# Recurrent attention, Mish layer and greedy experts: later bonuses on VectorE, a gate that counts four columns at a time, and its branch behind the experts

## The chip, the cores and the metric

The kernel runs on one core of a Trainium2 chip. Its engines have queues of their own: TensorE (PE; its weight loads are PEld), VectorE (DVE), ScalarE (ACT), GpSimd (POOL), and SyncE (SP), which issues most transfers; POOL issues the gathers and scatters. They meet at semaphores. The metric is the device time of one execution in microseconds.

## The reference

Three stages follow one another. The first is a linear recurrence over 768 steps for 4 x 8 heads of width 48, the second a dense layer over 3072 tokens, the third a mixture of 8 experts, where each token goes to one expert and each expert takes 384 tokens, picked greedily by the size of the logits.

```python
for t in range(S):
    cur = np.einsum('bhd,bhe->bhde', u[None] * kt, vt)
    y[:, :, t] = np.einsum('bhd,bhde->bhe', rt, state + cur)
    state = wt[:, :, :, None] * state + np.einsum('bhd,bhe->bhde', kt, vt)

h = x @ w_in
g = h * np.tanh(np.log1p(np.exp(h)))            # h above 20 is taken as it is
x = g @ w_out

order = np.argsort(-(x @ w_gate).flatten())
for idx in order:                               # largest logit first
    tok, e = idx // E, idx % E
    if assigned[tok] >= 0 or counts[e] >= cap: continue
    assigned[tok] = e; counts[e] += 1
for e in range(E):
    out[assigned == e] = np.maximum(x[assigned == e] @ w1[e], 0) @ w2[e]
```

The term with `u` is the bonus: step t's own key and value enter y with the weight sum over d of r*u*k, one number for each token and head.

## The kernel before

All matmuls of the two layers run on float16 halves: each operand is split into a high and a low part, and three products (high*high, high*low, low*high) stand for one. One list of events, sorted by keys from a table of numbers (`CFG`), fixes the order in which the instructions are written out; each engine works through its own in that order.

*Attention.* The sequence is cut into 24 units of 128 rows (two batches of 64 steps). A unit goes through the steps `att0`, `r1`, `k1` (decays, scaled r and k on VectorE), `bon1`, `bon2` (the bonus), `K`, `A1`, `S`, `y`. For the bonus, `att0` multiplies r and k of the unit in their transposed layout (line 353), `bon1` sums over d with eight small float32 matmuls against `u_T` (line 374) and moves the result to SBUF (`bT`), `bon2` transposes it on TensorE (line 381), moves it again (`bt`) and spreads it over a diagonal `Dt` (line 387). `CFG["dve"]` says for which units or pieces VectorE and for which ScalarE does such a move.

*Dense layer.* 12 groups of 256 tokens; `mm1` (line 561) makes the hidden tiles, VectorE and ScalarE the activation, and `mm2` (line 616) the output, in a stream of steps (`mm2_stream`): a step is three matmuls of 128x384, or 128x392 where eight columns carry the gate's logits. The stream's steps are strewn between the other work as fillers (`more(n)`); how many remain for the gate is set by `CFG["rate"]` and `CFG["beat"]`.

*Gate* (`gate`, `count`). Instead of sorting, seven phases look for the threshold at which the next expert is full, by 32-way search: four rounds in the first phase, three in each later one, 22 counts. In a count VectorE compares the tokens' values with 32 grid points (`compare`, two halves, line 839), TensorE adds up, by 24 matmuls of 32 columns of weights, how many tokens of each expert lie above each point (`tally`, line 844), VectorE compares with the free places (`ge`, line 858), TensorE spreads the result to all partitions (line 861) and VectorE takes the maximum (line 862). At each `yield` fillers from the stream are put in, `CFG["amount"]` steps of three. `aside` holds pieces of VectorE work (the low half of the first expert's weights, line 1095; the assignment of the last phase) that are put into a count, one at a time.

*Indices* (`make_idx`). A token's slot is turned into two one-hot matrices, `Q` (slot over 128) and `OH` (slot modulo 128, times the token's number), whose product over 24 matmuls is the list of tokens by expert; `check` counts whether every expert has 384. Then the first gathers go out, every engine loads the check's result into a register (line 1206) and branches (line 1207) around `exact_gate`, which is run when the check fails. Thirty dummy matmuls (`hold`, line 1214) stand ahead of the experts.

*Experts.* For each of 8: gather the rows (line 1116), transpose (1128), two matmul layers (1150, 1167), scatter (1172), with the next expert's weights split in between.

Of the kernel before, what the change touches and what calls it, by code (L numbers as in the profile page):

```python
# [18 lines left out]
P = 128  # L19
# [4 lines left out]
CFG = {'conv': [-28.468, -27.682, -10.675, -9.847, -2.299, 2.231, 3.277, 4.9, 3.919, 5.933, 7.595, 7.755, 8.526, 9.471,  # L24
          10.454, 11.547],
 'split': [-25.675, -27.076, -3.646, 1.639, 1.676, 2.567, 3.66, 7.281, 4.908, 7.502, 8.011, 9.047, 9.415, 10.573,
           10.811, 12.671],
 'ogT': [5.845, 8.719, 9.555, 9.756, 11.048, 11.752, 12.058, 13.442],
 'ogM': [7.704, 9.381, 9.717, 10.657, 11.711, 12.133, 12.863, 15.308],
 'u': ({'att0': -6.475,  # L30
        'bon1': -2.417,
        'bon2': -1.013,
        'r1': 0.465,
        'k1': -1.596,
        'K': 1.584,
        'A1': 2.502,
        'S': 3.903,
        'y': 3.747},
       {'att0': -2.581,
        'bon1': -0.459,  # L40
        'bon2': 0.009,
        'r1': -0.43,
        'k1': 0.751,
        'K': 5.062,
        'A1': 5.181,
        'S': 5.915,
        'y': 5.938}),
 'un': {0: {'att0': -24.666,
            'r1': -16.321,
            'bon1': -15.996,  # L50
            'k1': -21.723,
            'K': -15.816,
            'A1': -14.582,
            'bon2': -15.13,
            'S': -15.595,
            'y': -13.813},
        1: {'att0': -20.054,
            'r1': -19.91,
            'bon1': -18.88,
            'k1': -18.572,  # L60
# [3 lines left out]
            'S': -16.313,  # L64
            'y': -15.386},
        2: {'att0': -21.397,
            'r1': -20.207,
            'bon1': -20.059,
            'k1': -19.864,
            'bon2': -3.587,  # L70
            'K': 4.356,
            'A1': 3.2,
            'S': 6.8,
            'y': 7.301},
        3: {'att0': -21.601,
            'r1': -18.499,
            'bon1': -0.615,
            'k1': -16.885,
            'bon2': 2.966,
            'K': 3.773,  # L80
            'A1': 6.657,
            'S': 6.652,
            'y': 7.118},
        4: {'K': 5.178,
            'A1': 4.914,
            'S': 5.604,
            'y': 8.165,
            'att0': 0.318,
            'bon1': 1.82,
            'bon2': 4.604,  # L90
            'r1': 3.684,
            'k1': 4.536},
        5: {'y': 7.557,
            'att0': -2.858,
            'bon1': 3.509,
            'bon2': 3.642,
            'r1': 3.498,
            'k1': 1.649,
            'K': 6.184,
            'A1': 5.986,  # L100
            'S': 6.749},
        6: {'att0': -3.536, 'bon1': -2.54, 'bon2': 0.136},
        7: {'att0': -2.822, 'bon1': -0.422, 'bon2': 1.839}},
 'rate': [(17, 1), (16, 18), (77, 192), (80, 194), (96, 224), (99, 245)],
 'beat': (16, 82, (8, 3, 1, 1, 1, 0, 3, 5)),
 'close_cv': 15.533,
 'close_att': 86.65,
# [11 lines left out]
           ('ld', 5): -25.319,  # L119
           ('ld', 6): -18.857,  # L120
           ('ld', 7): -23.785,
           ('ld', 8): -21.26,
           ('ld', 9): -20.908,
           ('warm', 1): -24.585,
           ('warm', 2): -22.903,
           ('warm', 3): -6.441,
           ('warm', 4): 9.117,
           ('warm', 5): 2.921,
           ('warm', 6): 3.3},
 'warm': [3, 0, 3, 21, 0, 2, 8],  # L130
 'amount': {'I0': 3, 'I1': 0, 'c': 3, 'g': 1, 'o': 20, 't': 5},
# [7 lines left out]
         'ghi': {2, 4, 5, 6, 7, 9, 10, 14, 17, 18, 19, 22, 26, 27, 30, 31, 34, 35, 38, 39, 42, 43, 46, 47},  # L139
# [7 lines left out]
 'alone': {9},  # L147
 'lg': 8.022,
 'hold': 30,
 'xq': set(),  # L150
 'cvn': 2}
# [3 lines left out]
def tile_rwkv_mish_greedy_moe(  # L155
# [3 lines left out]
    v: bass.AP,  # L159
    u: bass.AP,  # L160
    w_in: bass.AP,
# [7 lines left out]
    NU, C, H, D = v.shape  # L169
# [44 lines left out]
    UN = [divmod(n, NCH) for n in range(NU)]  # L214
    vt = {}
# [17 lines left out]
    def load_v(n):  # L233
        if n >= NU:
            return
        vt[n] = pa.tile([P, H, D], F32, name="v")
        nc.sync.dma_start(vt[n], v[n])
# [19 lines left out]
    u_T = pa.tile([P, NP, 2, 32], F32, name="u_T", bufs=1)  # L257
    nc.sync.dma_start(u_T.rearrange("p a h b -> p (a h b)"), u)
# [82 lines left out]
    def att0(n):  # L341
# [10 lines left out]
        rk = pa.tile([P, NP, C], F32, name="rk", bufs=1)  # L352
        nc.vector.tensor_tensor(rk, Tps["r", n], Tps["k", n], op=ALU.mult)
        rks[n] = rk
# [14 lines left out]
    def bon1(n):  # L369
        pb = pq.tile([P, C], F32, name="Y", bufs=2)  # L370
        for h in range(2):
            t = slice(L * h, L * h + L)
            for p in range(NP):
                nc.tensor.matmul(pb[32 * p:32 * p + 32, t], u_T[:, p, h, :], rks[n][:, p, t], start=True, stop=True)
        bTs[n] = pa.tile([P, C], F32, name="bT", bufs=1)
        move("bT", n, bTs[n], pb)

    def bon2(n):
        pb = pq.tile([P, C], F32, name="Y", bufs=2)
# [3 lines left out]
        move("bT", n, bt, pb.rearrange("t (p j) -> t j p", j=32)[:, 0:2, :])  # L383
        bt = bt.rearrange("t j p -> t (j p)")
# [222 lines left out]
    def mm2_part(g, m, f, n):  # L607
# [7 lines left out]
        for i, (a, b) in enumerate(((0, 0), (0, 1), (1, 0))):  # L615
            nc.tensor.matmul(x, gt[:, a, ff, m * P:(m + 1) * P], wo[:, b, f, 0:n],  # L616
                             start=(f == 0 and i == 0), stop=(f == NF - 1 and i == 2))

# [41 lines left out]
    def mm2_stream():  # L660
        for g in range(NG):
            for m in range(MG):
                for f in range(NF):
                    mm2_part(g, m, f, WO if g < ND0 else DM)
# [52 lines left out]
    def more(n):  # L717
        for _ in range(n):
            next(fill, None)
        done[0] += n  # L720
# [56 lines left out]
    J = 32  # L777
# [46 lines left out]
    cnS = pgt.tile([J, NE], F32, name="cnS")  # L824
    ohj = pgt.tile([J, J], F32, name="ohj")
# [16 lines left out]
    def tally(cn, E_, h):  # L842
        for i in range(h * QT, (h + 1) * QT):
# [476 lines left out]
```

## Time and profile before

| what | value |
|---|---|
| runs shown | 783.0, 784.49, 786.48 us, median 784.49 |
| profiled execution | 783.24 us, span of its instructions 781.5 us |
| PE busy | 733.1 us, 94% of the span |
| DVE busy | 556.6 us, 71% |
| ACT busy | 411.0 us, 53% |
| POOL busy | 57.0 us, 7% |
| mean granted clock of TensorE | 0.981 of full speed |

The span is what the trace covers. Matmuls overlap, so a group's length is read from its start to the start of the next group; its own figure runs to a modelled end and is longer. The weight loads run beside the matmuls.

### The profile page before, as it was taken

How to read it: one execution, taken by the hardware profiler on the slowest of the kernel's cores; microseconds unless marked ns; L12 is line 12 of the kernel's file. 1: busy time of each engine (PE TensorE's matmuls, PEld its weight loads, DVE VectorE, ACT ScalarE, POOL GpSimd, SP SyncE). 2: the span in 40 equal slices, each digit the busy share in tenths (PEclk: the TensorE clock that was granted, in tenths of full speed). 3: DMA queues.
4: the chain of work that ended last, by engine and by line, in shares of the span. 5: the costliest groups of instructions: out<-in, count | busy, mean ns of one | idle time of the engine just before them, and what ended most of it. 6: DMA issues, size and time to landing. Idle time of an engine off the chain costs nothing. (4 is left out here: it accounts for less than half of the span.)

```text
span 781.5 us, 20165 instructions
## 1 busy us (share of the span) xinstructions
PE 733.1 (94%) x8807; PEld 517.0 (66%) x8807; DVE 556.6 (71%) x1054; ACT 411.0 (53%) x689; POOL 57.0 (7%) x98
## 2 busy tenths in 40 slices
PE   3977699999999999999999999999979999999996
PEld 2656576878777787777777765555556666666663
DVE  8999996978788887978777446777745664446620
ACT  3365875576774667667576781110024565445621
POOL 0000000000000000000000010000031223312211
PEclk9998899999999999999999999999989999999999
DMA  8852331323133141322210005100525644456100
GB/s 335 247 181 60 125 97 26 68 42 86 45 67 60 40 94 41 70 57 47 53 27 13 5 14 180 22 21 12 183 74 182 213 150 162 167 200 212 52 31 30
DMA packets 22220, 74.12 MB, mean 95 GB/s; under 512 B 4496, under 2 KB 13072, under 8 KB 20080
## 3 DMA queue, kind: packets, MB, share of 16 engines
q1 hardware_dynamic: 19056, 63.35, 27.7%
q0 software_dynamic: 3072, 9.44, 3.8%
q8 instruction: 71, 1.16, 0.6%
q14 instruction: 21, 0.17, 0.1%
HBM read 62.15 MB, written 9.44 MB: 92 GB/s over the span
## 5 line engine op out<-in xcount | busy, mean ns | idle before, releaser
L561 PE MATMUL Hp<-xg,wi 128*128 128x256 f16 x1728 | 210.4, 277 | 3.9 <-ACT wi L504 1.9
L616 PE MATMUL X<-wo,g 128*128 128x392 f16 (+1 forms) x1152 | 211.0, 328 | 0.0
L561 PEld LDWEIGHTS <-wi 128*128 128x128 f16 x1728 | 167.8, 99 | 33.3 <-ACT wi L504 2.1
L616 PEld LDWEIGHTS <-g 128*128 128x128 f16 x1152 | 107.2, 98 | 63.5 <-issue 0.9
L565 ACT ACTIVATE es<-Hp 128x512 f32<-128x512 f32 x96 | 57.4, 597 | 112.8 <-PE Hp L561 80.0
L1167 PE MATMUL X<-a,hT 128*128 128x384 f16 x576 | 97.2, 326 | 0.0
L1150 PEld LDWEIGHTS <-a 128*128 128x128 f16 x612 | 57.8, 98 | 37.2 <-issue 1.2
L1167 PEld LDWEIGHTS <-hT 128*128 128x128 f16 x576 | 56.4, 98 | 34.8
L1150 PE MATMUL Hp<-xe,a 128*128 128x384 f16 (+1 forms) x468 | 74.7, 314 | 0.7 <-DVE xe L1131 0.4
L588 DVE TENSOR_TENSOR hs<-hs,es 128x1024 f32<-128x1024 f32 x48 | 57.6, 1218 | 17.8 <-ACT es L580 17.6
L601 DVE TENSOR_TENSOR g<-hs,g 128x1024 f16<-128x1024 f32 x48 | 58.7, 1224 | 13.1 <-ACT g L329 12.1
L1095 DVE SCALAR_TENSOR_TENSOR a<-stg,a 128x384 f16<-128x384 f32 (+1 forms) x112 | 63.9, 607 | 0.0
L1092 ACT ACTIVATE a<-stg 128x384 f16<-128x384 f32 (+1 forms) x112 | 56.9, 561 | 0.8 <-DMA stg<-in_w_dram 0.8
L1170 ACT ACTIVATE or<-X 128x384 f32<-128x384 f32 x24 | 11.8, 491 | 81.0 <-issue 60.7
L1155 DVE SCALAR_TENSOR_TENSOR hT<-Hp,hT 128x384 f16<-128x384 f32 x48 | 26.4, 551 | 38.7 <-ACT hT L1154 38.7
L1131 DVE SCALAR_TENSOR_TENSOR xe<-cn,xe 128x384 f16<-128x384 f32 x24 | 13.2, 553 | 56.4 <-ACT xe L1130 56.4
L580 ACT ACTIVATE es<-es,right 128x1024 f32<-128x1024 f32 x48 | 53.3, 1153 | 0.2
L329 ACT ACTIVATE x1o<-X 128x384 f32<-128x384 f32 x19 | 9.4, 493 | 81.2 <-PE X L616 41.6
L329 ACT ACTIVATE hs<-Hp 128x512 f32<-128x512 f32 x77 | 46.0, 598 | 9.0 <-DVE g L601 9.0
L573 ACT ACTIVATE es<-es,mid__124 128x2048 f32<-128x2048 f32 x24 | 48.1, 2003 | 0.4
L1116 POOL DMA_INDIRECT xr<-x_dram,idx x24 | 27.5, 1146 | 119.6 <-DVE idx L1067 111.4
L273 ACT ACT_TABLE_LOAD x26 | 33.4, 1283 | 1.2 <-PEq L1304 0.8
(190 smaller groups left out, 881.1 us busy)
## 6 DMA issues: line engine op xcount, KB each, us to landing
stg<-in_w_dram SPq DMA_DIRECT2D x16, 1536.0 KB, 6.8
T<-in_rkw_dram SPq DMA_DIRECT2D x42, 289.5 KB, 4.9
g<-in_w_out_dram SPq DMA_DIRECT2D x8, 768.0 KB, 5.8
v<-in_v_dram SPq DMA_DIRECT2D x24, 192.0 KB, 3.1
x_dram<-x1o SPq DMA_DIRECT2D x48, 96.0 KB, 2.2
g<-in_w_in_dram SPq DMA_DIRECT2D x4, 768.0 KB, 7.9
wo<-in_w_in_dram SPq DMA_DIRECT2D x4, 768.0 KB, 11.6
xg<-xg SPq DMA_DIRECT2D x72, 16.0 KB, 1.9
```

The lines of the kernel that those rows point to most:

```text
L329: nc.scalar.activation(dst, src, AF.Copy, scale=scale)
L561: nc.tensor.matmul(h[:, fi, :], wi[:, a, kk, f * P:(f + 1) * P], xg[g][:, b, kk, :], start=(n == 0), stop=(n == 3 * KD - 1))
L565: nc.scalar.activation(es[g, hf][:, 2 * q:2 * q + 2, :], h, AF.Tanh, scale=0.5 / (SX * SWI))
L573: nc.scalar.activation(e, e, AF.Arctan, scale=-0.5, bias=mid_)
L580: nc.scalar.activation(e, e, AF.Sin, scale=-2.0, bias=right)
L588: nc.vector.tensor_tensor(h, h, e, op=ALU.mult)
L601: (nc.vector if on_v("glo", 2 * H_ + q) else nc.gpsimd).tensor_tensor(gt[:, 1, sl], h, gt[:, 0, sl], op=ALU.subtract)
L616: nc.tensor.matmul(x, gt[:, a, ff, m * P:(m + 1) * P], wo[:, b, f, 0:n], start=(f == 0 and i == 0), stop=(f == NF - 1 and i == 2))
L1092: nc.scalar.activation(dst[:, 0], src, AF.Copy, scale=sc_)
L1095: nc.vector.scalar_tensor_tensor(dst[:, 1], src, sc_, dst[:, 0], op0=ALU.mult, op1=ALU.subtract)
L1150: nc.tensor.matmul(ps[:, cs], a1[:, a, kk, f * P:(f + 1) * P], x[:, b, kk, cs], start=(n == 0), stop=(n == 3 * KD - 1))
L1167: nc.tensor.matmul(ps, h[:, a, f, ms], a2[:, b, f, :], start=(n == 0), stop=(n == 3 * NF2 - 1))
```

## The change

1. Units 6 to 23 (`nb` is 6) no longer compute their bonus on TensorE. r and k of such a unit are loaded a second time, in the layout with tokens on partitions (`rkn`, 128 x 768 floats, one buffer; `u` repeated on all partitions in `uw`); VectorE multiplies r by k, by u, and sums over d.
2. A count's tally takes four token columns at once: six matmuls with 128 columns of weights and 32 moving columns give all pairs of four, `own` masks the pairs that belong together (a VectorE product into `cm`), and four matmuls with `fold` add the four quarters up. The fillers are now given by single matmuls (`more_third`), with one more place for them (`s`). `aside` pieces stand behind `cm`, or behind `ge` where a phase begins.
3. Index lists use slots over 64 and modulo 64; the token's number goes into `Q`.
4. The register is loaded ahead of the last expert and the branch stands behind it; its body repeats the experts. `check` stands behind the indices, and 70 dummy matmuls where 30 were.
5. The table of numbers is another one throughout (keys, fillers, who does which move).

```diff
- 'amount': {'I0': 3, 'I1': 0, 'c': 3, 'g': 1, 'o': 20, 't': 5},
+ 'amount': {'I0': 8, 'I1': 1, 'c': 8, 'g': 2, 's': 2, 'o': 33, 't': 12},
...
     def bon1(n):
+        if n >= NB:
+            return
...
     def bon2(n):
+        if n >= NB:
+            x = rkn[n]
+            nc.vector.tensor_tensor(x[:, 0], x[:, 0], x[:, 1], op=ALU.mult)
+            nc.vector.tensor_tensor(x[:, 0], x[:, 0], uw, op=ALU.mult)
+            bt = pa.tile([P, 2, NP], F32, name="bt")
+            for j in range(2):
+                nc.vector.tensor_reduce(bt[:, j], x[:, 0].rearrange("t (p j d) -> t j p d", p=NP, j=2)[:, j], op=ALU.add,
+                                        axis=AX.X)
+            rkn.pop(n)
+            load_rk(n + 1)
+            bonus_diag(n, bt)
+            return
...
+    nc.vector.tensor_copy(fold, ident[:, 0:J])
+    for i in range(4):
+        nc.vector.tensor_reduce(own[:, i, 0:1], ident[:, J * i:J * i + J], op=ALU.max, axis=AX.X)
+        if i:
+            nc.vector.tensor_tensor(fold, fold, ident[:, J * i:J * i + J], op=ALU.add)
+        nc.vector.tensor_copy(own[:, i, 1:NE], own[:, i, 0:1].to_broadcast([P, NE - 1]))
...
     def tally(cn, E_, h):
-        for i in range(h * QT, (h + 1) * QT):
-            nc.tensor.matmul(cn, I_[:, i, :], E_[:, i, :], start=(i == 0), stop=(i == NTT - 1))
+        for i in range(h * QT, (h + 1) * QT, 4):
+            nc.tensor.matmul(cn, I_[:, i:i + 4, :], E_[:, i:i + 4, :], start=(i == 0), stop=(i == NTT - 4))
...
-            if h == NH - 1 and aside:
-                aside.pop(0)()
             yield f"I{h}"
-            tally(cn, E_, h)
+            tally(c4, E_, h)
+        nc.vector.tensor_tensor(cm, c4, own, op=ALU.mult)
         if late is not None:
             late()
+        elif aside:
+            aside.pop(0)()
+        yield "s"
+        cn = pgs.tile([P, CAP], F32, name="hx", bufs=1)[0:J, 0:NE]
+        for i in range(4):
+            nc.tensor.matmul(cn, fold, cm[:, i * NE:(i + 1) * NE], start=(i == 0), stop=(i == 3))
         nc.vector.tensor_tensor(ge, cn, remS[0:J, :], op=ALU.is_ge)
+        if late is not None and aside:
+            aside.pop(0)()
         yield "g"
...
+        nc.vector.tensor_tensor(Q, Q, tid[:, :, None].to_broadcast([P, NTT, 2 * NTT]), op=ALU.mult)
...
-            for i in range(q * NTT // NQ, (q + 1) * NTT // NQ):
-                nc.vector.tensor_scalar(OH[:, i], col, slf[:, 1, i:i + 1], tid[:, i:i + 1], op0=ALU.is_equal, op1=ALU.mult)
+            i = slice(q * NTT // NQ, (q + 1) * NTT // NQ)
+            nc.vector.tensor_tensor(OH[:, i], col[:, None, 0:64].to_broadcast([P, NTT // NQ, 64]),
+                                    slf[:, 1, i, None].to_broadcast([P, NTT // NQ, 64]), op=ALU.is_equal)
...
-    redo = nc.values_load(badi, min_val=0, max_val=NE)
-    with tc.If(redo > 0):
-        exact_gate()
-        run_through(make_idx())
-        gather(0)
...
+    experts(lambda: redo.append(nc.values_load(badi, min_val=0, max_val=NE)))
+    with tc.If(redo[0] > 0):
+        exact_gate()
+        run_through(make_idx())
...
+        gather(0)
+        experts()
```

**VectorE around a later unit's diagonal.** Before (`L387` is the diagonal; its `bt` comes from TensorE by way of ScalarE; `L353` is the r*k product):

```order
L350 SCALAR_TENSOR_TENSOR F_144<-T_93,first 128x520
L353 TENSOR_TENSOR rk<-T_93 128x512
L601 TENSOR_TENSOR g<-hs,g 128x1024
L327 TENSOR_SCALAR hs<-Hp 128x512
L458 TENSOR_TENSOR S_142<-S_146,Y 128x4x48 x2
L460 TENSOR_TENSOR S_142<-S_142,F_140 128x8x48
L327 TENSOR_SCALAR xg<-A 128x4x128
L480 SCALAR_TENSOR_TENSOR xg<-A,xg 128x4x64 x2
L397 TENSOR_TENSOR T_92<-T_92,F_140 128x512
L387 TENSOR_TENSOR Dt<-diag,bt 128x512
```

and now, at the same place of the program (`rk` is the tile with tokens on partitions):

```order
L491 TENSOR_TENSOR S_142<-S_146,Y 128x4x48 x2
L493 TENSOR_TENSOR S_142<-S_142,F_140 128x8x48
L339 TENSOR_SCALAR xg<-A 128x4x128
L513 SCALAR_TENSOR_TENSOR xg<-A,xg 128x4x64 x2
L430 TENSOR_TENSOR T_93<-T_93,F_140 128x512
L397 TENSOR_TENSOR rk<-rk 128x384
L398 TENSOR_TENSOR rk<-rk,uw 128x384
L401 TENSOR_REDUCE bt<-rk 128x4 x2
L420 TENSOR_TENSOR Dt<-diag,bt 128x512
```

The r*k product left its place behind the scan, and four instructions that read only loaded data stand directly ahead of the diagonal.

**VectorE in one count of the first phase.** Before (`I_` the compare, `a` a piece of the weights, `ge` the comparison with the free places, `sc` the maximum):

```order
L839 TENSOR_TENSOR I__6877<-best,jk_6837 128x384 x2
L1095 SCALAR_TENSOR_TENSOR a_6907<-stg,a_6907 128x512
L858 TENSOR_TENSOR ge<-cn,remS 32x8
L862 TENSOR_REDUCE sc<-tp 128x1
L909 TENSOR_SCALAR y<-best,sc 128x24
```

and now:

```order
L887 TENSOR_TENSOR I__6718<-best,jk_6678 128x384 x2
L902 TENSOR_TENSOR cm<-cn,own 128x32
L1154 SCALAR_TENSOR_TENSOR a_6763<-stg,a_6763 128x512
L911 TENSOR_TENSOR ge<-hx,remS 32x8
L917 TENSOR_REDUCE sc<-tp 128x1
L964 TENSOR_SCALAR y<-best,sc 128x24
```

The masking product `cm`, which waits for the tally, now stands ahead of the piece of the weights, and `ge` behind both.

**TensorE at the end of the index lists.** Before:

```order
L1065 LDWEIGHTS OH
L1065 MATMUL cn<-Q,OH 128x24
L1206 TENSOR_LOAD badi
L1207 COMPARE_AND_BRANCH
L844 LDWEIGHTS I__6877
L844 MATMUL cn<-Eo,I__6877 32x8
```

and now:

```order
L1123 LDWEIGHTS OH
L1123 MATMUL cn<-Q,OH 64x24
L1011 LDWEIGHTS ones
L1011 MATMUL tp<-cp,ones 128x8
L1268 LDWEIGHTS ones
L1268 MATMUL cn<-tri,ones 128x128
```

The load and the branch around the exact gate (whose first tally stands behind them before) are gone from here; the check's matmul and the dummy matmuls follow the last index matmul directly.

In the program as written out, the stream holds 393 fillers between the first reduction of the range and the experts before, and 396 now.

## Rows read from the trace of the kernel before

**Rows 1.** Busy us (and count) in two stretches: PE, PEld, DVE, ACT, POOL; clock; DMA
```profile
40.00:120.00 80.00, 61.48 (x1026) 49.99 (x1025) 77.24 (x120) 57.06 (x93) 0.00 (x0) 0.87 0.38 111
160.00:450.00 290.00, 288.77 (x4261) 222.70 (x4259) 230.15 (x350) 194.03 (x272) 0.00 (x0) 1.00 0.22 49
```

**Rows 2.** Timeline of PE around one unit's bonus: start us, us, instruction
```profile
319.51 0.43 PE L374 MATMUL Y<-rk,u_T 128*32 128x64 f32 x16
319.87 2.14 PE L561 MATMUL Hp<-xg,wi 128*128 128x256 f16 x18
...
324.98 0.27 PE L381 MATMUL Y<-ident,bT 128*128 128x128 f32 x1
325.09 1.66 PE L616 MATMUL X<-wo,g 128*128 128x392 f16 x9
```

**Rows 3.** Groups of VectorE by form: count, busy us, mean ns, idle before
```profile
L353 DVE TENSOR_TENSOR rk<-T 128x512 f32<-128x512 f32 x24 | 16.0, 667 | 0.5 <-DMA T<-in_rkw_dram 0.5
...
L460 DVE TENSOR_TENSOR S<-S,F 128x384 f32<-128x384 f32 x20 | 11.2, 558 | 0.7
...
L920 DVE TENSOR_REDUCE best<-M 128x24 f32<-128x192 f32 x7 | 2.3, 334 | 0.0
```

**Rows 4.** Timeline where the gate begins
```profile
477.54 0.16 DVE L871 SCALAR_TENSOR_TENSOR wk<-wk 128x1 f32<-128x1 f32 x1
...
478.93 0.27 PE L874 MATMUL tp<-ident,wk 128*1 128x128 f32 x1
```

**Rows 5.** Timeline of one count of the gate
```profile
487.44 0.76 PE L844 MATMUL cn<-Eo,I__6877 128*32 128x8 f16 x24
487.47 0.69 DVE L1095 SCALAR_TENSOR_TENSOR a<-stg,a 128x512 f16<-128x512 f32 x1
...
488.23 0.15 DVE L858 TENSOR_TENSOR ge<-cn,remS 32x8 f16<-32x8 f32 x1
...
488.72 0.17 PE L861 MATMUL tp<-ge,ones 32*128 32x8 f16 x1
...
489.48 1.03 DVE L839 TENSOR_TENSOR I__6877<-y,jk 128x384 f16<-128x384 f32 x2
...
490.40 0.76 PE L844 MATMUL cn<-Eo,I__6877 128*32 128x8 f16 x24
```

**Rows 6.** Timeline: small matmuls with 128 columns of weights
```profile
103.92 0.60 PE L537 MATMUL Y<-wgs,wT 128*128 128x8 f16 x18
```

**Rows 7.** Timeline from the last count to the experts; then landing of the gathers
```profile
558.16 0.17 PE L861 MATMUL tp<-ge,ones 32*128 32x8 f16 x1
...
564.54 0.76 DVE L1054 TENSOR_TENSOR Q<-col,slf 128x576 f16<-128x576 f16 x1
...
571.41 0.18 DVE L1067 TENSOR_SCALAR idx<-sl 128x24 int32<-128x24 int32 x1
...
573.98 0.96 POOL L1116 DMA_INDIRECT xr<-x_dram,idx  x1 [0.30 <-issue]
575.09 3.29 PE L1214 MATMUL cn<-OH,ones 128*128 128x128 f16 x30 [3.93 <-PEq L1207]
578.21 0.83 PE L1128 MATMUL cn<-ident,xr 128*128 128x128 f32 x6
...
DMA to landing us min/median/max: 3.0/3.4/4.3
```

**Rows 8.** Register loads and branches: ns min/median/max, first and last start us
```profile
L1206 PEldq TENSOR_LOAD <-badi x1: 492/492/492, 571.0 to 571.0; - x1
...
L1207 ACTq COMPARE_BRANCH  x1: 50/50/50, 567.8 to 567.8; - x1
...
L1207 PEldq COMPARE_BRANCH  x1: 3359/3359/3359, 571.6 to 571.6; - x1
```

**Rows 9.** The last scatter (timeline), and POOL's drain at the end
```profile
775.68 0.96 POOL L1172 DMA_INDIRECT out_dram<-or,idx  x1 [2.85 <-ACT or L1170]
...
L1315 POOLq DRAIN  x3: 40/113/5199, 775.4 to 781.2; - x3
```

More of the change, by code (lines that the diff above doesn't have):

```diff
@@ L103 @@
[L103 to L106, printed above, removed]
+            'S': -16.335,
+            'y': -15.249},
+        2: {'att0': -21.418,
+            'r1': -19.974,
+            'bon1': -19.617,
+            'k1': -19.64,
+            'bon2': -3.61,
+            'K': 4.997,
+            'A1': 3.276,
+            'S': 6.922,
+            'y': 7.451},
@@ new lines @@
+        3: {'att0': -21.269,
+            'r1': -17.288,
+            'bon1': -0.568,
+            'k1': -15.337,
+            'bon2': 3.561,
+            'K': 3.783,
+            'A1': 6.667,
+            'S': 6.009,
+            'y': 7.234},
+        4: {'K': 5.214,
+            'A1': 4.95,
+            'S': 5.604,
+            'y': 7.836,
+            'att0': 0.608,
+            'bon1': 1.856,
+            'bon2': 4.294,
+            'r1': 3.706,
+            'k1': 4.57},
+        5: {'y': 7.485,
+            'att0': -2.727,
+            'bon1': 3.512,
+            'bon2': 3.756,
+            'r1': 3.755,
+            'k1': 1.907,
+            'K': 6.014,
+            'A1': 5.811,
+            'S': 6.972},
@@ L158, in tile_rwkv_mish_greedy_moe @@
     rkw: bass.AP,
-    v: bass.AP,
+    rkv: bass.AP,
     u: bass.AP,
+    ur: bass.AP,
     w_in: bass.AP,
@@ L1064, in make_idx @@
             for i in range(q * NTT // NQ, (q + 1) * NTT // NQ):
-                nc.tensor.matmul(ix, OH[:, i, :], Q[:, i], start=(i == 0), stop=(i == NTT - 1))
+                for b in range(2):
+                    nc.tensor.matmul(ix[64 * b:64 * b + 64], OH[:, i, :], Q[:, i, b::2], start=(i == 0),
+                                     stop=(i == NTT - 1), skip_group_check=True)
         nc.vector.tensor_scalar(sl, ix, float(-(NT // 2)), float(NT - 1 - NT // 2), op0=ALU.max, op1=ALU.min)
@@ L1193, in tile_rwkv_mish_greedy_moe @@
     for kind in gate():
-        more(amount[kind])
+        more_third(amount[kind])
     while aside:
         aside.pop(0)()
-    for kind in make_idx(check):
-        more(amount[kind])
+    for kind in make_idx():
+        more_third(amount[kind])
+    check()
     more(1000)
@@ L1205, in tile_rwkv_mish_greedy_moe @@
     gather(0)
-    redo = nc.values_load(badi, min_val=0, max_val=NE)
-    with tc.If(redo > 0):
-        exact_gate()
-        run_through(make_idx())
-        gather(0)
-    if CFG["hold"]:
-        hold = pgs.tile([P, P], F32, name="cn")
-        for _ in range(CFG["hold"]):
-            nc.tensor.matmul(hold[:, 0:P], ones, OH[:, 0], start=True, stop=True)
+    hold = pgs.tile([P, P], F32, name="cn")
+    for _ in range(CFG["hold"]):
+        nc.tensor.matmul(hold[:, 0:P], ones, tri, start=True, stop=True)
     pend = {}
@@ L1226, in more_cv, with experts @@
                 conv_lo(*x)
-    for e in range(NE):
-        nx = e + 1 < NE
-        f = 0
-        while f < NF2:
-            k = 2 if e == 0 and f == 0 else 1
-            e_mm1(e, *range(f, f + k), parts=ME if k > 1 else 1)
-            for i in range(f, f + k):
-                if i == 0 and nx:
-                    gather(e + 1)
-                    if e > 0:
-                        load_w(e + 1)
-                if nx:
-                    more_cv(e + 1)
-            f += k
-        more_cv(e + 1, 100)
-        for m in range(ME):
-            if nx:
-                xpose(e + 1, m)
-            e_mm2(e, m)
+    def experts(last=None):
+        for e in range(NE):
+            nx = e + 1 < NE
+            if not nx and last is not None:
+                last()
+            f = 0
+            while f < NF2:
+                k = 2 if e == 0 and f == 0 else 1
+                e_mm1(e, *range(f, f + k), parts=ME if k > 1 else 1)
+                for i in range(f, f + k):
+                    if i == 0 and nx:
+                        gather(e + 1)
+                        if e > 0:
+                            load_w(e + 1)
+                    if nx:
+                        more_cv(e + 1)
+                f += k
+            more_cv(e + 1, 100)
+            for m in range(ME):
+                if nx:
+                    xpose(e + 1, m)
+                e_mm2(e, m)
+    redo = []
+    experts(lambda: redo.append(nc.values_load(badi, min_val=0, max_val=NE)))
+    with tc.If(redo[0] > 0):
+        exact_gate()
+        run_through(make_idx())
+        for d in (pend, wts, wf, xe, hT):
+            d.clear()
+        scat.clear()
+        load_w(0)
+        for x in small_pieces(0):
+            conv_hi(*x)
+            conv_lo(*x)
+        load_w(1)
+        gather(0)
+        experts()
 _OUTS = [((3072, 384), "float32")]
```

204 lines of the change are left out of this document (99 added, 105 removed), and 27 rows, old and new, of the table CFG.

## The prediction

> **What bounds the kernel now.** I read the busy time by stretch first. From 160 to 450 us TensorE is busy for 288.8 of 290 us at the full clock, VectorE for 230 [rows 1]: there time is TensorE work, and a microsecond taken off it is a microsecond. From 40 to 120 us it is the other way round, VectorE 77.2 of 80 and TensorE 61.5 [rows 1]; the change keeps the first six units' bonus as it is and adds nothing to VectorE before that point, so I give this part no gain and no loss. Then the timelines of three places: a unit's bonus, one count of the gate, and the passage from the gate to the experts, where TensorE stands.
>
> **The change part by part.**
>
> *The bonus of units 6 to 23.* In the stream of TensorE the eight products of one unit take from 319.51 to 319.87, 0.36 us, and its transpose from 324.98 to 325.09, 0.11 us [rows 2]. That is 0.47; the durations modelled for the two are 0.43 and 0.27, 0.70 together, but they overlap with their neighbours. I take 0.50 a unit, near the stream's figure: 18 x 0.50 = 9.0 us, all on the engine that bounds. What VectorE takes over: two products of 128x384 at 0.56, two sums over 192 numbers at 0.33, less the 0.67 of the old r*k product [rows 3]: 1.12 + 0.67 - 0.67 = 1.1 us a unit, 20 us in all, of which the new table hands some 7 back to ScalarE (nine moves of the hi half and two of kn, 128x512 each, at the 0.67 of such an instruction [rows 3]). VectorE has 60 us to spare in 160 to 450 [rows 1], so I price this at nothing; with that cover gone the wait could eat the whole 9. At the other end stands 18 x 0.70 = 12.6 us. The r and k rows that are loaded anew are on no path: a load for unit n+1 goes out behind the sums of unit n, some ten of VectorE's instructions ahead of its reader. Behind it on SP's queue stand x1's stores and the loads of later units, which are not due then.
>
> *The gate's start.* Twelve small VectorE instructions that make `fold` and `own` now stand between the read of the last logits and the two reductions of the range. Nothing shows them; by the 0.16 of the smallest one there [rows 4] they are 1.9 us. So the maximum that TensorE transposes is ready at about 479.7 and not at 477.70, where 15 fillers covered it until 478.93 [rows 4]. Twelve fillers end 0.5 earlier: TensorE waits about 1.3 us, and the first compare comes 0.4 us later than before, with seven fillers fewer spent. Bounds -1 (the twelve hidden) to +0.9.
>
> *The 22 counts.* Before, a count takes 2.96 us (487.44 to 490.40), 12 fillers of it [rows 5]. A filler is 0.163 us (nine with 392 columns take 1.66 with one 0.33 us tail [rows 2], scaled to 384). The 24 matmuls are 0.69 us. Their six successors have 128 columns of weights; the nearest row is 18 matmuls of that kind with 8 columns in 0.60, less a tail of 0.17, so 0.025 each [rows 6]. I take 0.17 for six and 0.11 for the four that fold: 0.4 us less TensorE time a count. But the chain grows by a link. From the start of the matmul that spreads the result (488.72) the second compare ends at 490.51, +1.79 [rows 5]. TensorE comes to the second half of the tally at +1.86 (eight fillers, three matmuls, one filler, two changes of 0.1), the masking product on VectorE runs until about +2.31 (0.19, between the 0.15 of a 32x8 instruction and the 0.55 of a 128x384 one [rows 5]), and behind it, ahead of the `ge` that the next matmul needs, stands a piece of the weights, 0.69 for 512 columns [rows 5] or 0.55 for 384 [rows 3]: `ge` ends at +3.12 and the next spread starts at +3.2. Of the sixteen counts that don't open a phase six go like this (+0.24), eight with the smaller piece (3.05, +0.09), two without (2.91): +2.1 us together, with 13 fillers each for 12. The six that open a phase come out even, 4.7 us, but their `assign` now follows `ge` and holds up the next reduction by 0.3: +1.8. Counts: +4 us, while 16 more fillers are done. Bounds: -2 (VectorE never late, TensorE sets 2.9 and the phase openings gain) to +11 (half a microsecond more a count).
>
> *Indices and the branch.* From the last spread (558.16) the indices are there at 571.59, +13.4, and the experts' first transposes start at 578.21, +20.05 [rows 7]. Up to Q (564.54, +6.38) nothing changes. Q grows from 576 to 1152 numbers: 0.76 plus 576 x 1.08 ns (the slope between the 0.55 of 384 and the 0.76 of 576), 1.38, and comes twice; four products of 384 at 0.48 a piece (1.03 for two [rows 5]) replace 24 instructions. Last one-hot at +11.0, indices at about +12.0. The gathers follow them as before: the second one was issued 2.4 us after the indices and lands 3.0 to 3.4 us later [rows 7], so its data are there at +17.4 to +17.8. TensorE no longer loads a register (0.49 us) and jumps (3.36 us) ahead of its dummy matmuls [rows 8]. Thirty of these took 3.29 us, 0.11 each, at half the clock [rows 7]; seventy, begun at +11.7, end between +15.5 (full clock) and +19.4 (half clock throughout). I take +18.0: 2.0 us gained, bounds 0.7 and 2.6. In total 396 fillers are left for gate and indices and not 393, 0.5 us less before it.
>
> *The end.* In front of the last expert TensorE reads the register, 0.49 us [rows 8], part of which the matmuls already queued hide: +0.3 (0 to 0.5). Behind the last store every engine now jumps. TensorE's 3.36 us begin with its last matmul, before the last store is even issued, and the program ends 5.8 us after that issue (775.68 to 781.5) with POOL's drain until 780.6 [rows 9], so this jump is covered. POOL adds a handful of semaphore instructions behind the last landing: +0.6, from 0 to 4 if its drain starts afresh.
>
> ScalarE's jump took 0.05 us, over a body with one instruction of its own; TensorE's over thousands took 3.36 [rows 8]. Now ScalarE and POOL jump over some 270 and 110 instructions. [...]
>
> Sum: -9.0 + 0.4 + 4.0 - 2.0 - 0.5 + 0.3 + 0.6 = -6.2 us. The profiled execution took 783.24 (span 781.5), so 777.0; it lies 1.25 below the median of the runs shown, 784.49, so I forecast 778.3.
>
> **The rivals.**
>
> *No room on VectorE.* Bonus and diagonal are now 2.5 us in one piece on VectorE, and it also serves TensorE's waits. For it: VectorE's share of 79% becomes some 85% (240 of 281). Against: TensorE has 1.2 us without work in 290 [rows 1], so the slack of each wait is large. If the waits eat 8.5 of the 9.0: 786.8, no change.
>
> *The gate's round trip decides (slower).* A count now crosses between TensorE and VectorE three times where it crossed twice. I let a crossing cost 0.06 to 0.1; the matmul behind `ge` started 0.34 us after it (488.38 to 488.72 [rows 5]), and whether fillers or the crossing made this can't be told. If the crossing costs this and the piece of weights ahead of `ge` its full length, a count loses 0.5 more: 22 x 0.5 = 11, 789.3. It decides from 0.46 us a count on (22 x 0.46 = 10.1, +3.9 over 784.49).
>
> *The gate gains what TensorE saves.* If pieces and masking fit beside the fillers, the 22 counts cost no time of their own: 4 us less, 774.3. For it speaks that `ge` ends 0.34 ahead of the matmul it feeds [rows 5]; against, the new order on VectorE's queue.
>
> *The end pays for the branch.* POOL's drain of 5.2 us restarts behind the new waits, or a jump comes after the last landing: 3.5 more, 781.8, no change.
>
> **How the numbers follow.** Forecast 0.50 (own range 775 to 781.5), no room 0.14, round trip 0.10, gate gains 0.16, the end 0.10. About 0.5%, 4 us, is what a measurement of this kernel can tell from no change: faster means under 780.6, slower over 788.4. Faster: 0.46 of the forecast, the 0.16, and little of the end: 0.64. Slower: 0.07 of the round trip and 0.03 of no room: 0.10. Same: 0.26. The range goes from 771.5 (the gate gains and the bonus gives its upper bound) to 786 and leaves out most of the round trip and the worse half of no room.
>
> **What would show it.** Right: the stretch up to the gate is 9 us shorter with TensorE still without idle time; a normal count takes 3.0 to 3.2 us, with VectorE's weight piece ending just before `ge`; TensorE's dummy matmuls start within 0.5 us of the last index matmul, and the experts' first transposes about 6 us after the indices; a register load of half a microsecond at the last expert. Wrong: waits of TensorE for VectorE between 160 and 450, counts of 3.5 us, a clock of one half when the experts begin, more than 6.5 us between the last store's issue and the end.

## The result and the profile after

Times are in us. The last five rows are of the profiled executions; the first tally of the gate, its last spread and the last scatter cut them into stretches.

| | before | after |
|---|---|---|
| median, 4 runs each | 785.19 us (783.0 to 786.48) | 772.42 us (771.84 to 773.37) |
| profiled execution, its span | 783.24, 781.5 | 772.55, 770.7 |
| first tally of the gate | 484.32 | 471.31 (-13.0) |
| last spread of the gate | 558.16 | 544.41 (-13.75) |
| issue of the last scatter | 775.68 | 761.62 (-14.06) |
| from there to the end of the span | 5.8 | 9.1 (+3.3) |

The ratio is 0.9841, 95% interval 0.9816 to 0.9867: 1.6% faster, about 12.5 us. The forecast was 778.3; the time lies below the forecast's own range (775 to 781.5) and just inside the wide one (771.5 to 786). The profiled execution of before lies 2 us under its median; so the two spans differ by 10.8 and not by 12.5.

The first two stretches again, for the kernel after (columns as in [rows 1]):

```profile
40.00:120.00 80.00, 63.99 (x1037) 51.76 (x1036) 77.09 (x120) 58.66 (x96) 0.00 (x0) 0.91 0.41 114
160.00:450.00 290.00, 286.61 (x4099) 221.70 (x4097) 238.37 (x380) 202.13 (x271) 2.71 (x16) 1.00 0.29 68
```

From 40 to 120 us VectorE is as full as before, and TensorE is busy for 2.5 us more of the same 80. In the later stretch TensorE, which waited 1.2 us of 290, now waits 3.4. The bonus of one unit on VectorE, in the timeline (start us, us, instruction), which stands where [rows 2] stood on TensorE:

```profile
315.16 0.55 DVE L397 TENSOR_TENSOR rk<-rk 128x384 f32<-128x384 f32 x1
315.75 0.56 DVE L398 TENSOR_TENSOR rk<-rk,uw 128x384 f32<-128x384 f32 x1
316.34 0.61 DVE L401 TENSOR_REDUCE bt<-rk 128x4 f32<-128x192 f32 x2
316.99 0.69 DVE L420 TENSOR_TENSOR Dt<-diag,bt 128x512 f32<-128x512 f32 x1
```

The four new instructions take 1.83 us of the engine (315.16 to 316.99), 33 us for 18 units, less 12 for the old r*k. The start of the gate, on VectorE and TensorE (answers [rows 4]):

```profile
464.26 0.17 DVE L866 CAST fold<-ident 128x32 f16<-128x32 f32 x1
464.34 0.18 DVE L868 TENSOR_REDUCE own<-ident 128x1 f32<-128x32 f32 x1
...
465.43 0.17 DVE L871 COPY own<-own 128x7 f32<-128x7 f32 x1
465.55 0.07 DVE L950 MEMSET rem<- 128x8 f32 x1
...
466.41 0.27 PE L929 MATMUL tp<-ident,wk 128*1 128x128 f32 x1 [0.31 <-DVE wk L926]
```

Twelve instructions of 0.17 to 0.18 us pass in 1.29 us, since the starts stand 0.08 to 0.22 apart; TensorE waits 0.31. One count of the gate (answers [rows 5]):

```profile
489.34 0.16 PE L916 MATMUL tp<-ge,ones 32*128 32x8 f16 x1
489.43 1.47 PE L649 MATMUL X<-wo,g 128*128 128x384 f16 x8
490.01 1.03 DVE L887 TENSOR_TENSOR I__6718<-y,jk 128x384 f16<-128x384 f32 x2
490.74 0.23 PE L892 MATMUL cn<-Eo,I__6718 128*128 128x32 f16 x3
491.10 0.24 PE L892 MATMUL cn<-Eo,I__6718 128*128 128x32 f16 x3
491.37 0.19 DVE L902 TENSOR_TENSOR cm<-cn,own 128x32 f16<-128x32 f32 x1 [0.33 <-PE cn L892]
491.48 0.68 DVE L1154 SCALAR_TENSOR_TENSOR a<-stg,a 128x512 f16<-128x512 f32 x1
491.62 0.24 PE L910 MATMUL hx<-cm,fold 128*32 128x8 f16 x4
492.08 0.15 DVE L911 TENSOR_TENSOR ge<-hx,remS 32x8 f16<-32x8 f32 x1
492.28 0.16 PE L916 MATMUL tp<-ge,ones 32*128 32x8 f16 x1
```

The count takes 2.94 us, with the piece of weights (L1154) between the masking product and `ge`, as foreseen. But `ge` starts 0.71 us after the masking product and not 0.19 + 0.69 later: again the steps from start to start (0.11 and 0.60) are shorter than the durations.

This count is one of the shorter. Of the 21 counts from the first spread to the last, fifteen open no phase; they take 2.89 to 3.11 us, 2.99 on average, and took 2.96 before, with one filler fewer. The six that open a phase do 21 fillers as before and got shorter by 0.24 to 0.27 us, spread to spread; one of them, before and after:

```profile
494.63 0.17 PE L861 MATMUL tp<-ge,ones 32*128 32x8 f16 x1
499.31 0.17 PE L861 MATMUL tp<-ge,ones 32*128 32x8 f16 x1
```

```profile
481.99 0.16 PE L916 MATMUL tp<-ge,ones 32*128 32x8 f16 x1
486.40 0.16 PE L916 MATMUL tp<-ge,ones 32*128 32x8 f16 x1
```

So from the first spread to the last, 72.39 us before and 71.45 now, the six give 1.5 us and the other counts take 0.6 back. The passage to the experts (answers [rows 7]):

```profile
553.46 1.96 DVE L1116 TENSOR_TENSOR OH<-col,slf 128x384 f16<-128x384 f16 x4
555.95 5.20 PE L1268 MATMUL cn<-tri,ones 128*128 128x128 f16 x70
556.23 0.18 DVE L1126 TENSOR_SCALAR idx<-sl 128x24 int32<-128x24 int32 x1
560.98 0.50 PE L1187 MATMUL cn<-ident,xr 128*128 128x128 f32 x3
563.29 0.55 PE L1187 MATMUL cn<-ident,xr 128*128 128x128 f32 x3 [1.82 <-remote]
566.24 3.30 PE L1209 MATMUL Hp<-xe,a 128*128 128x128 f16 x36
```

The indices come 12.0 us after the last spread, the dummy matmuls start at +11.5 and end at +16.6; then TensorE stands 1.82 us for the second gather. At the end, register loads, branches and POOL's last instructions (ns min/median/max, first and last start; answers [rows 8, 9]):

```profile
L1306 PEldq TENSOR_LOAD <-badi x1: 486/486/486, 734.3 to 734.3; - x1
...
L1307 POOLq EVENT_SEMAPHORE  x5: 17/43/43, 761.9 to 764.7; - x5
...
L1307 PEldq COMPARE_BRANCH  x1: 3559/3559/3559, 757.7 to 757.7; - x1
L1307 ACTq COMPARE_BRANCH  x1: 50/50/50, 760.9 to 760.9; - x1
...
L1307 ACTq EVENT_SEMAPHORE  x1: 17/17/17, 763.5 to 763.5; - x1
...
L1307 POOLq INC_SWDGE_SEM  x1: 1144/1144/1144, 764.7 to 764.7; - x1
...
L1390 POOLq DRAIN  x3: 40/107/3997, 765.9 to 770.5; - x3
```

POOL's long drain took 5.2 us before and began at 775.4, with the last scatter. Now the branch's semaphores stand ahead of it, the last of them 3.0 us behind that scatter's issue; the drain begins 4.3 us after the issue and takes 4.0. The jumps themselves are covered: TensorE's 3.56 us ends at 761.3. ScalarE's branch over some 270 instructions shows 50 ns, but its next event comes 2.6 us later (760.9 to 763.5); no row shows what fills them.

### The profile page after: what moved, and what is told of

Read it like the earlier page. It is cut to its first block, busy times and chain, and to the rows that moved or that the text cites. A ratio compares the mean times of both kernels' runs of the same rounds, so it can differ in the third digit from the quotient of the medians.

```text
span 770.7 us, 19203 instructions
## 1 busy us (share of the span) xinstructions
PE 720.9 (94%) x8272; PEld 504.1 (65%) x8272; DVE 568.4 (74%) x1106; ACT 414.0 (54%) x677; POOL 57.3 (7%) x98
## 4 chain that ended last, share of the span: by engine, by line
PE 38%; DVE 26%; issue 20%; ACT 6%; POOL 6%; DMA 3%; SPq 0%; another core or an unknown queue 0%; POOLq 0%; DVEq 0%; ACTq 0%
PE X L649 16%; PE Hp L594 11%; POOL xr L1175 3%; DVE g L634 3%; DMA T<-in_rkw_dram 3%; POOL out_dram L1231 2%; DVE hs L621 2%; DVE E L373 2%; DVE F L362 2%; DVE cv L530 2%; DVE cv L531 1%; PE Hp L1209 1%; ACT es L606 1%; PE A L447 1%; PE X L1226 1%
## 5 line engine op out<-in xcount | busy, mean ns | idle before, releaser
L649 PE MATMUL X<-wo,g 128*128 128x392 f16 (+1 forms) x1152 | 214.9, 328 | 0.0
L594 PE MATMUL Hp<-xg,wi 128*128 128x256 f16 x1728 | 207.6, 275 | 2.6 <-DMA xg<-xg 1.4
L649 PEld LDWEIGHTS <-g 128*128 128x128 f16 x1152 | 105.5, 98 | 62.7 <-issue 1.9
L1154 DVE SCALAR_TENSOR_TENSOR a<-stg,a 128x384 f16<-128x384 f32 (+1 forms) x112 | 64.1, 611 | 0.0
```

The source lines that it names most:

```text
L594: nc.tensor.matmul(h[:, fi, :], wi[:, a, kk, f * P:(f + 1) * P], xg[g][:, b, kk, :], start=(n == 0), stop=(n == 3 * KD - 1))
L1154: nc.vector.scalar_tensor_tensor(dst[:, 1], src, sc_, dst[:, 0], op0=ALU.mult, op1=ALU.subtract)
```

## The experiments

All are told by their ratio to the kernel before, measured beside it; a per cent is 7.85 us, and the half-widths of the intervals are 1.2 to 3.3 us. Single profiled executions of the same program up to the gate have their first tally at 471.05 to 473.25 (four kernels), so differences of 2 us there mean nothing.

**1. The bonus back on TensorE, in the changed kernel.**

```
- 'nb': 6}
+ 'nb': 24}
```

> The changed kernel, but all 24 units keep their bonus on TensorE; order table, gate and branch as in the changed kernel. Theory A (the 12.9 us that the first tally of the gate comes earlier are the bonus): 18 units x 0.5 to 0.7 come back on TensorE, the first tally goes from 471.3 to 480 to 484, the time from 772.4 to 781.5 to 785. Theory B (the rewritten order table made the part that is there already at 150 us, some 7.5 us): only the rest comes back, the first tally at 476 to 477, the time about 778.

801.82 us, ratio 1.0226 (1.0184 to 1.0268). Neither theory: 17.7 us slower than the kernel before. The longest wait of TensorE from 160 to 440 us (total, times, longest), and one of the six in the timeline:

```profile
PE Y L484 <- ACT bT L341: 13.8, 6, 2.3
```

```profile
256.91 0.60 ACT L341 ACTIVATE hs<-Hp 128x512 f32<-128x512 f32 x1 [2.38 <-DVE g L634]
257.41 0.27 ACT L341 ACTIVATE bT<-Y 128x128 f32<-128x128 f32 x1
257.73 0.67 PE L484 MATMUL Y<-v,kn 64*64 64x48 f32 x30 [2.30 <-ACT bT L341]
```

Line 484 is a product of step `S`. It writes to `Y`, of which there are two buffers, and one of them holds the sums of `bon1` until ScalarE has copied them to `bT`. That copy stands in ScalarE's queue behind one that waits for VectorE. Here the product comes 1.3 us after `bon1` (253.83 to 255.17); in the kernel before, 18 matmuls of the first layer lie between ([rows 2], from 319.87). The run measures a misfit and not the bonus. The 13.8 us are the largest wait and not the whole loss: the first tally comes at 503.8.

**2. The bonus left out**, once in the kernel before (TensorE's products and transpose, and the moves), once in the changed kernel (VectorE's products and sums).

```
before:                               after:
 def bon1(n):                          if n >= NB:
+    if n >= 6: return                -    (two products, two sums, loads)
 def bon2(n):                         +    nc.gpsimd.memset(bt, 0.02)
+    if n >= 6: memset(bt, 0.02)           bonus_diag(n, bt)
```

> The kernel before, where the units 6 to 23 leave the bonus out on TensorE (the eight products, the transpose and the two moves between them; a constant stands in its place; r*k on VectorE stays). Theory A (the prediction's term: 0.5 us a unit on the engine that bounds): 9 us less, 776 to 777. Theory B (the modelled durations are the price, 0.7 a unit): 12.6 less, 773. Theory C (in the old order something else sets the time, as it seems from the changed kernel in the old order, which gained nothing ahead of the gate): 782 to 785.

777.27 us, ratio 0.9894 (0.9862 to 0.9927): 8.3 us less, nearest to theory A. TensorE's busy time up to the first tally falls from 449.1 to 439.5, 0.53 a unit.

> The changed kernel, where the units 6 to 23 leave out VectorE's part of the bonus too (two products and two sums a unit, and the loads of their rows; a constant stands in its place). Theory A (VectorE has room, the 36 products and 36 sums cost nothing): first tally at 470.5 to 471.3, the time 771.5 to 772.5. Theory B (VectorE's 32 us are in part on the path): 766 to 770.

769.16 us, ratio 0.9803 (0.9772 to 0.9834), 3.0 us below the changed kernel by the two ratios, whose intervals overlap. Its first tally is at 467.9, 3.2 us earlier than in the earliest of the four other executions. From 160 to 440 us TensorE is busy (second figure) for 277.0 of 280 in the changed kernel and for 279.8 without the 72 instructions:

```profile
160.00:440.00 280.00, 277.00 (x3991) 214.76 (x3989) 235.74 (x375) 192.21 (x261) 0.00 (x0) 1.00 0.30 70
```

```profile
160.00:440.00 280.00, 279.76 (x4018) 217.22 (x4016) 210.98 (x317) 196.72 (x264) 1.35 (x13) 1.00 0.23 51
```

So VectorE's part costs about 3 us, theory B at its lower end, though VectorE is idle for 44 of those 280. The loads of its rows are left out with it, but none of TensorE's waits in this stretch of the changed kernel is put down to a load. There are seven, 3.0 us in all, 1.8 for VectorE and 1.2 for ScalarE; without the 72 instructions 0.2 are left. The largest for VectorE stands behind a bonus and its diagonal, which had VectorE from 348.28 to 350.71:

```profile
351.98 0.28 PE L679 MATMUL Hp<-g,wo 128*8 128x256 f16 x4 [0.68 <-DVE g L634]
```

How the bonus makes the six others is not shown one by one.

**3. The order table, whole and in halves.** With the bonus on VectorE, the new gate and the branch at the end: all times, dummy matmuls and shares of the old table; the old shares alone (`dve`); the old times alone. And the new shares in the kernel before.

```
 c = dict(CFG_before); c['amount'], c['hold'], c['nb'] = after's      # all old
 c = dict(CFG_after);  c['dve'] = CFG_before['dve']                   # old shares
 c = dict(CFG_before); c['amount'], c['hold'], c['nb'], c['dve'] = after's   # old times
 c = dict(CFG_before); c['dve'] = CFG_after['dve']        # before, new shares
```

> The changed kernel (bonus of 18 units on VectorE, new gate, branch at the end) with the order table, the dummy matmuls of the start and the shares of VectorE of the kernel before. Theory A: the table hardly matters, the time is 772 to 775 and the first layer is as far at 150 us as in the changed kernel. Theory B: the early gain is the table's, the first 144 matmuls of the first layer are passed at 72 us and not at 68, the first tally comes 6 to 8 us later, the time is 778 to 780.

> The changed kernel with VectorE's share of the moves as in the kernel before (nine more moves of x's hi half and two of kn on VectorE, the rest of the sets too), and all other numbers of the order as in the changed kernel. Theory A (the shares made the early gain, by freeing VectorE where it bounds): first tally at 478 to 481, the time 779 to 782. Theory B (the order's times made it): first tally at 471 to 474, the time 772 to 775.

> The changed kernel with the order's times and dummy matmuls of the kernel before, but VectorE's share of the moves as in the changed kernel (the opposite half of the run with the old shares). Theory A (the new shares make room on VectorE for the bonus, the times add little): first tally at 472 to 476, the time 773 to 777. Theory B (times and shares only serve together): first tally at 480 to 485, the time 779 to 784.

> The kernel before with VectorE's share of the moves as in the changed kernel, all else as it was: the bonus stays on TensorE. Theory A (the shares relieve VectorE, which bounds from 40 to 120 us, bonus or no bonus): first tally 3 to 5 us earlier, 780 to 782. Theory B (they only pay for the bonus on VectorE; where TensorE bounds they are worth nothing): 784 to 786.

| shares | times | bonus | median | ratio (95%) |
|---|---|---|---|---|
| old | old | VectorE | 780.33 | 0.9932 (0.9907 to 0.9958) |
| old | new | VectorE | 783.23 | 0.9978 (0.9963 to 0.9994) |
| new | old | VectorE | 783.01 | 0.9992 (0.9975 to 1.0010) |
| new | new | VectorE (the changed kernel) | 772.42 | 0.9841 (0.9816 to 0.9867) |
| new | old | TensorE (before) | 784.73 | 0.9998 (0.9981 to 1.0016) |

The table as a whole is worth 7.1 us (0.9932 to 0.9841), and neither half of it gives anything without the other; without the new bonus the shares give nothing either. Theory B holds, within 0.4 us, in the first, third and fourth of these runs; with the old shares the time lies 1 us above theory A. The new times in the kernel before were not tried. The stretch from 160 to 440 us with all old, with the old shares and with the old times:

```profile
160.00:440.00 280.00, 273.72 (x3925) 209.29 (x3923) 238.07 (x386) 182.67 (x235) 0.00 (x0) 0.99 0.30 71
```

```profile
160.00:440.00 280.00, 271.87 (x3918) 208.35 (x3916) 235.47 (x382) 181.17 (x236) 0.00 (x0) 0.99 0.29 70
```

```profile
160.00:440.00 280.00, 272.96 (x3944) 211.02 (x3943) 234.11 (x377) 191.14 (x256) 0.00 (x0) 0.99 0.30 71
```

TensorE stands still for 6.3, 8.1 and 7.0 us, in the changed kernel for 3.0 and in the kernel before for 1.2. VectorE is busy for 234 to 238 in all four: so its total does not tell them apart. That the difference lies in when its instructions come is argued, not shown. Part of the table's gain lies ahead of this stretch: the 432nd matmul of the first layer starts at 161.4 us in the kernel before, at 160.3, 156.4 and 159.3 in these three, and at 154.1 in the changed kernel. (The execution with all old that was profiled took 783.42, the longest of its six; its place in this row of three is not exact.) Which of the table's numbers does it was not tried.

**4. The old tally.** 24 matmuls a count, no masking, no fold, twelve fillers.

```
- for i in range(h * QT, (h + 1) * QT, 4):
-     nc.tensor.matmul(cn, I_[:, i:i + 4, :], E_[:, i:i + 4, :], ...)
+ for i in range(h * QT, (h + 1) * QT):
+     nc.tensor.matmul(cn, I_[:, i, :], E_[:, i, :], ...)
```

> The changed kernel with the 24 matmuls of the old tally, without the masking product and the four folding matmuls, twelve fillers a count. Theory A (a count lasts as long as the chain of VectorE and TensorE, about 2.95 us, in both forms): spread to spread 2.95 to 3.0, first to last spread about 72, the time within 1.5 us of 772.4. Theory B (the prediction's sum: a count grew by its longer chain, 4 us in all): about 768. Theory C (TensorE's work sets a count): 22 x 0.3 to 0.4 more, 779 to 781.

774.95 us, ratio 0.9870 (0.9850 to 0.9890): 2.3 us slower than the changed kernel by the ratios, whose intervals overlap. First to last spread 72.39 us and not 71.45, counts of 2.95 and 4.68. The spreads are as theory A has them. But of the 2.3 only 0.9 lies between them. The old form does 17 fillers fewer from the first tally to the last spread (309 for 326). Seven of them are done ahead of the first tally, 1.1 us at 0.163, and ten among the indices; there the first gather is issued 14.8 us after the last spread and not 13.0, since it waits for the store of the last rows:

```profile
561.62 1.13 POOL L1158 DMA_INDIRECT xr<-x_dram,idx  x1 [111.89 <-DMA x_dram<-x1o]
```

From the first tally to the last scatter only 0.6 us of all this is left (290.9 for 290.3), as the experts begin faster here: their run of 36 matmuls takes 2.49 us, 3.30 in the changed kernel. So what the new tally by itself is worth is not clear of noise. Theory B falls, C's price too; and theory A's reason is wrong, as run 6 shows.

**5. The branch back in the middle**, behind the first gathers; then the check it reads made earlier; then with fewer dummy matmuls.

```
 gather(0)
+redo = nc.values_load(badi, min_val=0, max_val=NE)
+with tc.If(redo > 0):
+    exact_gate(); run_through(make_idx()); gather(0)
 hold = ...                         # 30 matmuls; second: make_idx(check); third: 16
```

> The changed kernel with the register load and the branch back behind the first gathers and thirty dummy matmuls behind them instead of seventy. Theory A (in front of the experts TensorE waits for the second gather, 563.3, whatever it does meanwhile; at the end the branch makes the program outlive the last store by 9.1 us and not 5.8): 0.5 + 3.4 + 3.3 us from about 556.0 end at 563.2, so nothing is lost there, and the end gives 3.3 back: 769 to 770. Theory B (as the prediction had it: the branch ahead of the experts costs 2 us, the one at the end 0.9): 773 to 774.

770.74 us, ratio 0.9811 (0.9791 to 0.9831). The end gives back its 3.3 us (last scatter 763.93, span 769.7), but the passage gets longer by 2.2 (94.1 us from the first tally to the transposes, where the second block's began at 92.0 in the changed kernel): the dummy matmuls run until 565.2, 6.8 us behind the second gather's issue (558.44).

```profile
561.00 3.25 PE L1273 MATMUL cn<-tri,ones 128*128 128x128 f16 x29 [5.27 <-PEq L1267]
...
565.19 1.51 PE L1187 MATMUL cn<-ident,xr 128*128 128x128 f32 x6
```

> As the run with the branch in the middle, and the check that the branch reads is made ahead of the one-hots again and not behind the indices. Theory A (there TensorE sat 5.3 us, 1.4 of them waiting for the check, and only then jumped): the register is read behind the last index matmul, the dummy matmuls begin at about 559.5 and end near 563, where the second gather lands: the experts begin 2 us earlier than in that run, 768 to 769. Theory B (the check's instructions delay the indices as much as they hasten the jump): 770 to 771.

771.92 us, ratio 0.9830 (0.9798 to 0.9863): no earlier than the run above within the intervals. From first tally to the experts' first transposes it takes 93.0 us instead of 94.1, where 2 were hoped for: the register is still loaded only behind the last index matmul, and the first check delays those. Up to the last scatter, again from the first tally, it is 2.3 us less than in the run above (290.6 for 292.9), but the first tally stands 2.2 us later, as far as single executions of one program differ. Theory A met in part.

> The run with the branch in the middle, with sixteen dummy matmuls behind the branch in place of thirty. Theory A (thirty of them at half the clock, 0.11 us each, outlast the second gather, which is there 4.4 us behind its issue, near 563): the experts' transposes start 1.5 to 2.2 us earlier against the first tally than with thirty, 769 to 769.5. Theory B (without them the experts begin at half the clock and lose the same again): 770.5 to 771.

769.46 us, ratio 0.9803 (0.9787 to 0.9819): theory A.

```profile
562.27 1.86 PE L1273 MATMUL cn<-tri,ones 128*128 128x128 f16 x16 [5.34 <-PEq L1267]
563.93 1.49 PE L1187 MATMUL cn<-ident,xr 128*128 128x128 f32 x6
```

The transposes start 91.65 us after the first tally (94.14 with thirty), 4.3 us behind the second gather's issue, and the run of 36 matmuls that follows soon takes 2.44 us; behind the seventy in the changed kernel it took 3.30, at a granted clock of 0.57 from 566 to 569 us:

```profile
566.00:569.00 3.00, 3.00 (x33) 2.93 (x32) 0.56 (x1) 0.49 (x1) 0.00 (x0) 0.57 0.24 69
```

This version is the fastest of those that compute the whole result, some 3 us below the changed kernel, though the two intervals just touch.

**6. More fillers in a count, fewer ahead of the gate**, with the branch in the middle and sixteen dummy matmuls.

```
- 'rate': [..., (80, 182), (96, 211), (98, 233)]    'I1': 1, 'g': 2
+ 'rate': [..., (80, 180), (96, 203), (98, 222)]    'I1': 2, 'g': 3
```

> As the run with the branch in the middle, with sixteen dummy matmuls behind it in place of thirty, fifteen fillers in a count in place of thirteen (one more before the second half of the tally, one more before the spread), and for it eleven fillers of three matmuls fewer ahead of the gate. Theory A (a count lasts as long as its chain over VectorE, TensorE has some 0.4 us to spare in it): spread to spread as before, 2.9 to 3.1 and 4.4, the first tally 5 us earlier, the experts begin about 2 us earlier than with thirty dummy matmuls: 763 to 766. Theory B (TensorE's work sets a count): 0.3 us more a count, 22 x 0.3 = 6.6 back: 769 to 771.

778.4 us, ratio 0.9929 (0.9908 to 0.9950): 9.9 us slower by the ratios than the run with sixteen dummy matmuls, from which it differs in these numbers alone. Both halves failed. The counts grew by some 0.16 us each:

```profile
494.52 0.17 PE L916 MATMUL tp<-ge,ones 32*128 32x8 f16 x1
497.61 0.17 PE L916 MATMUL tp<-ge,ones 32*128 32x8 f16 x1
```

First to last spread is 74.95 us (+3.5) for 42 fillers more, 6.8 us of matmuls: half of a filler is free, half is paid. And ahead of the gate the first tally comes at 475.27, later and not earlier, though 24 fillers fewer are done before it: the fillers taken away had covered waits. The stretch from 440 us to the first tally shows 5.7 us without work on TensorE, 2.4 in the changed kernel. After four waits from 458 to 464 us, 4.1 us together, the granted clock was 0.50 from 465 to 470 us, and twelve fillers took 3.76 us that take 2.11 in the changed kernel, whose clock is 1.00 over its whole stretch from 440 us:

```profile
440.00:475.27 35.27, 29.54 (x247) 17.78 (x244) 17.83 (x43) 18.71 (x22) 3.19 (x16) 0.90 0.29 102
```

```profile
465.00:470.00 5.00, 5.00 (x19) 2.87 (x18) 2.12 (x19) 2.71 (x5) 0.00 (x0) 0.50 0.59 246
```

```profile
466.77 3.76 PE L649 MATMUL X<-wo,g 128*128 128x384 f16 x12
```

## Why the prediction was right in direction and half the size

- **The bonus on TensorE, -9.0.** Confirmed: 8.3 us by the run that leaves it out of the kernel before.
- **VectorE's part, "at nothing".** This step failed, by 3 us in the new table (run 2). Spare time in the sum (60 us in 290) was read as cover, but TensorE waits at single places, one of them for an instruction of VectorE that stands behind 2.5 us of bonus and diagonal. With the old table TensorE stood still for 6.3 us of the stretch. The rival of no room was right in its mechanism, not in its size.
- **"I give this part no gain and no loss", and the moves handed to ScalarE counted only as VectorE's relief.** This is the term that was missing: the rewritten table, 7.1 us (run 3). I read its share sets as a refund of VectorE's time. With the old table the same change gives 0.9932 and not 0.9841. The early stretch, to which I gave no gain, is part of it: the 432nd matmul of the first layer starts at 154.1 to 156.1 us in the four kernels with the same program up to the gate, and at 161.4 before.
- **The gate's start, +0.4, and the 22 counts, +4.0.** Mis-sized, and of the wrong sign. From VectorE's read of the last logits to the first tally it takes 7.1 us and took 7.6: the twelve instructions need 1.29 us and not 1.9. First to last spread fell by 0.9 us. The order of links was right, and most counts lie in or near the 3.0 to 3.2 forecast, but I added durations of VectorE's instructions where their starts stand 0.08 to 0.1 us closer; in the count shown `ge` ended at +2.89 and not at +3.12. A crossing from VectorE to TensorE, put at 0.06 to 0.1, shows 0.06 where TensorE waits for `cp` of the indices, before (562.03 to 562.09) and after (548.28 to 548.34). The openings took 4.41 to 4.43 and not 4.7 and 0.3 more; the counts' whole gain is theirs. The rival that the gate gains what TensorE saves was half right: the counts cost no time, but run 6 shows that neither the chain nor TensorE alone sets a count, and its 774.3 owes its nearness to the measured 772.4 to terms that it left as they were.
- **Indices and the branch, -2.0.** Indices at +12.0 as worked out. The transposes of the second block began at +18.9 and not at +18.0: the second gather released TensorE 4.5 us after its issue (558.82 to 563.29) and not 3.4, and TensorE idled 1.8 us behind its seventy matmuls. Then its granted clock fell to 0.57 (566 to 569 us), and the matmuls behind the first run of 36 start 0.3 us earlier than before, counted from the last spread, and not 2.0 (569.38 and 583.44).
- **The load at the last expert, +0.3.** Its 486 ns do not show as idle time.
- **The end, +0.6.** +3.3: the rival that POOL's drain restarts. The 0.6 was an estimate that no row gave; the semaphore work of POOL took 1.14 us, and the drain began behind it. The jumps were covered: TensorE's, as argued, ended at 761.3, and ScalarE's next event came at 763.5, ahead of the drain at 765.9.

Up to the first tally 9.1 us were forecast (-9.0 - 0.5 + 0.4) and 13.0 came; from there to the last scatter 2.3 of loss (4.0 - 2.0 + 0.3) and 1.1 of gain; at the end 0.6 and 3.3 of loss. The errors went both ways: the table and the counts brought some 12 us more than forecast, the bonus, VectorE, the passage and the end some 8 less. That the total still lies inside the range is in part luck.

## What to carry to other kernels

When work moves to an engine with spare time, count the waits it causes in order, not the spare time; and a rewritten order table is a change of its own, to be priced or tried apart, since here it was worth nearly as much (7.1 us) as the work that was moved (8.3). In a chain of short instructions take the steps from start to start out of the timeline; durations overstated the count shown by 0.23 us. A branch moved off a busy passage isn't free at the end of the program, where it cost 3.3 us here: look at what it makes wait there.

## What was not expected of the hardware

- A branch behind the last stores made POOL do 1.14 us of semaphore work and begin its 4.0 us drain only behind it; in the kernel before, the 5.2 us drain ran from the last scatter on.
- Seventy dummy matmuls ended 1.8 us too early and the experts ran at 0.57 of the clock for 3 us; sixteen at a granted clock of 0.50 (561 to 565 us), which ended 4.3 us behind the second gather's issue, left 0.68 from 565 to 568 us and 1.00 from 568 to 571.
